# A GFNet-style spectral filter and a mixer MLP on one core: stages pinned to other units, block products in a fifth group, sums moved from GpSimd to VectorE, two loads moved

## The chip, the core and the metric

The kernel runs on one core of a Trainium2 chip. The core has a matrix engine (TensorE, PE in the profile; its weight loads are the row PEld), three engines for elementwise work (VectorE, DVE; ScalarE, ACT; GpSimd, POOL), a queue that issues DMAs (SyncE, SP), an on-chip memory of 128 partitions (SBUF) and eight accumulator banks (PSUM), into which only TensorE multiplies and which GpSimd doesn't reach in this kernel. The metric is the device time of one execution in microseconds; less is better.

## The reference

One input `x` of 2048 tokens by 448 channels is normalised (LayerNorm) and goes through two branches. Their results are added to `x`.

```python
x = A_x
xn = _layernorm(x, axis=-1)
return x + _A_ref(xn, A_w_r, A_w_i) + _B_ref(xn, B_w1, B_w2, B_w3, B_w4)
```

Branch A is a two-dimensional real Fourier transform over tokens and channels, a product with a complex filter of 2048 x 225, and the inverse transform. Branch B is an MLP mixer:

```python
h = _gelu(_layernorm(x, axis=-1) @ w1)            # 448 -> 448
...                                               # four quarters of h shifted by +1, -1, +2, -2 tokens
hs = jnp.concatenate([g0, g1, g2, g3], axis=-1) @ w2
x1 = x + hs
h2 = _gelu(_layernorm(x1, axis=-1) @ w3) @ w4     # 448 -> 1792 -> 448
return x1 + h2
```

## The kernel before, in words

**Numbers.** Every matrix product is made of halves: an fp32 operand is split into a high and a low fp16 part, and three products (high x high, high x low, low x high) are summed in PSUM. The elementwise engines make these splits: ScalarE writes the high part, VectorE the low one.

**Tiling.** The tokens are dealt into 16 blocks of 128 (token index = 16 a + b, block b). Blocks are grouped by four for the first layers of branch B (`GRP`) and by two for its large MLP: group G (0 to 7) holds blocks 2G and 2G + 1, 256 tokens. The 1792 hidden channels are cut into seven pairs of 128, fp = 0 to 6. A *unit* (G, fp) is made of a `front` (first layer: 22 matmuls of 256 columns at L435, then GELU and the split on ScalarE and VectorE, L773 to L777) and a `back` (second layer with w4, added into accumulators over the seven fp).

**Two ways of doing `back`.** A plain unit does 12 matmuls of 448 columns (L811). A *crossed* unit, for the groups listed in `STR` (5, 6, 7 before), does the high x high products plainly (4 matmuls of 448 columns, L811) and takes the two mixed products together as a 2 x 2 block product with seven instead of eight multiplications (Strassen-Winograd): 14 matmuls of 224 columns (L826). For that it needs sums and differences of the blocks of h (`forms`, three VectorE sums a unit, L786 to L788, into `hgm`), of w4 (`w4_forms`, once for each fp, into `w4x` and the end of the w4 tile), and at the end of a group two extra accumulators, which ScalarE copies out (L843), and six group sums (L846, L850). In the last group (G = 7) the units fp = 5 and 6 are plain.

**Branch A in stages.** `do_fold` (x normalised on ScalarE, L578, then four sums on GpSimd, L583 to L586), `step1_in` (split, L594 and L595) and `step1` (transform over a, 24 matmuls for a pair of blocks, L604) go pair by pair of blocks, eight times. `w_scale` takes the largest magnitude of the filter (eight loads, eight `absmax` reductions, L269). Then 16 *chunks* of frequencies pass through `chunk_a` (transform over channels), `chunk_b` (transform over b and product with the filter), `chunk_z` and `chunk_c` (first inverse step). At last the *inverse blocks* run: `gather_u`, `inv_a`, `inv_b`, one for each of the 16 blocks, and `finish` writes the output.

**What sets the order.** The program is written in one order and a planner deals it out to the engines' queues by priorities and its own estimate of times. Each engine then runs its queue strictly in order. Two tools steer the planner. `prio(FILL)` gives work of the large MLP the last priority, so that it fills TensorE wherever nothing else is ready, and `prio(EVAC)` gives what empties its accumulators the first. `behind(key)` pins work to a place: the instructions may be issued only after those that `key` names, ("f", G, fp) for the end of a front's splits, ("m", G, fp) for the last matmul of a back, ("s", n) for the n-th half unit, ("h", g, i) for the transposing DMA of block i of group g. A pin is an earliest place, not a time. The lists at the head of the file hold these places: `FOLD` and `PACE` (start of a pair's fold, its step 1), `WMAX` (the eight maxima), `LATE` (LayerNorm of the last four blocks, `ln2`), `units` with `INV` and `LAG` (inverse blocks). `AH = 2`: fronts run two units ahead of the backs.

Before, the units of G1 and G2 carry the folds, those of G3 and the first of G4 the chunks (a chunk every 7/3 half-unit steps from the start of G3), and the inverse blocks go one to a unit from (4, 4) on, with `inv_b` two units behind `inv_a`. The sums of `w4_forms` run on GpSimd, as do the group sums of G5 and G6; those of G7 run on VectorE.

**Loads.** All DMAs are issued by SP in its own order. The program starts with x, w1, w2 and w3 (w3 in four pieces, `load_w3`, L217 and L219), and `do_fold` loads a pair of x blocks for each fold (L574) into one of four buffers; the fourth is a part of `hgm`, which is free from the start. The `h` of the first layers is turned by transposing DMAs (L492), and so are later operands (L910 into `w4x`, L553 into `x2mem`).

## Time and profile before

| | |
|---|---|
| median of 3 runs | 410.05 us (409.68 to 412.14) |
| profiled execution | 409.72 us |
| its span, first to last instruction | 407.6 us |
| TensorE busy | 401.3 us (98%), 3379 matmuls |
| VectorE, ScalarE, GpSimd busy | 304.2, 268.6, 179.8 us |
| moved by DMA | 49.46 MB, mean 121 GB/s |
| granted TensorE clock | 0.999 |

Times in the rows are microseconds from the first instruction; a row of the groups reads: line, engine, operation, what it writes and reads, shape, count, then busy time and mean nanoseconds of one, then idle time of that engine before it and what ended it. A row of the chain of work that ended last has start, length, and what ran. The busy time of TensorE is modelled at the end of each matmul, so neighbouring matmuls overlap in it; the chain's pieces are cut where the next one starts.

### The profile page before, as it was taken

The numbers are of one execution on the slowest core, as the hardware profiler recorded it, in microseconds if no ns is written. First come the engines' busy times: TensorE is split into PE (matmuls) and PEld (weight loads), VectorE is DVE, ScalarE is ACT, GpSimd is POOL, SyncE is SP. The second block draws the span as 40 slices with busy tenths as digits, with TensorE's granted clock in tenths as the row PEclk, the third lists the DMA queues.
The fourth block names the chain that finished last, engine by engine and source line by source line (L and its number), as shares of the span: only waits on it lengthen the run. The fifth ranks groups of instructions, "written<-read, shape, count | busy, mean of one in ns | idle before, by whom it ended". The sixth has DMA issues, their size and how long they took to land.

```text
span 407.6 us, 8828 instructions
## 1 busy us (share of the span) xinstructions
PE 401.3 (98%) x3379; PEld 296.0 (73%) x3379; DVE 304.2 (75%) x658; ACT 268.6 (66%) x465; POOL 179.8 (44%) x276
## 2 busy tenths in 40 slices
PE   8998999999999999999999999999999999999996
PEld 4553555666767777776888887877788888888885
DVE  5988999899653757894577777763488879889645
ACT  4698993884737865763488888785956566544332
POOL 3889723011197747499243344441231254217100
PEclk9999999999999999999999999999999999999999
DMA  8999999915910375317055666642000022323201
GB/s 282 351 274 198 177 180 261 260 23 109 207 48 0 92 233 175 103 36 170 19 135 146 151 145 151 153 112 60 2 2 2 24 68 75 108 70 112 92 2 45
DMA packets 57209, 49.46 MB, mean 121 GB/s; under 512 B 41312, under 2 KB 52192, under 8 KB 57168
## 3 DMA queue, kind: packets, MB, share of 16 engines
q1 hardware_dynamic: 57168, 48.91, 46.4%
q8 instruction: 26, 0.43, 0.5%
q14 instruction: 15, 0.12, 0.1%
HBM read 35.06 MB, written 3.67 MB: 95 GB/s over the span
## 4 chain that ended last, share of the span: by engine, by line
PE 96%; DMA 2%; ACT 1%; DVE 0%; issue 0%; ACTq 0%
PE pw L435 33%; PE acc L811 24%; PE pw L510 9%; PE pw L465 6%; PE cr L826 4%; PE acc L826 3%; PE pu L707 3%; PE ps L604 3%; PE pp L661 2%; PE pe L727 2%; PE px L678 2%; PE py L749 2%; PE wps L889 2%; DMA h<-hs 2%; PE pta L414 1%; PE end L811 1%
## 5 line engine op out<-in xcount | busy, mean ns | idle before, releaser
L435 PE MATMUL pw<-x2mem,w3p 128*128 128x256 f16 x1232 | 149.7, 272 | 0.0
L435 PEld LDWEIGHTS <-w3p 128*128 128x128 f16 x1232 | 118.7, 98 | 19.4
L811 PE MATMUL acc<-w4p,hf 128*128 128x448 f16 x508 | 107.4, 352 | 0.0
L811 PEld LDWEIGHTS <-hf 128*128 128x128 f16 x532 | 51.5, 98 | 35.5
L777 DVE SCALAR_TENSOR_TENSOR hf<-pw,h,hf 128x512 f16<-128x512 f32 x56 | 41.8, 747 | 36.5 <-ACT hf L776 36.3
L773 ACT ACTIVATE pw<-pw,pe 128x512 f32<-128x512 f32 x56 | 36.7, 656 | 44.8 <-PE pw L435 44.6
L510 PE MATMUL pw<-w2p,h 112*128 112x448 f16 x192 | 39.2, 353 | 1.3 <-DMA h<-hs 1.2
L734 POOL TENSOR_TENSOR e<-e 128x226 f32<-128x226 f32 x16 | 11.1, 696 | 63.7 <-ACT e L731 56.2
L776 ACT ACTIVATE hf<-pw,h 128x512 f16<-128x512 f32 x56 | 38.3, 683 | 1.3
L465 PE MATMUL pw<-w1p,w4x 128*128 128x448 f16 x176 | 34.8, 352 | 0.5 <-DVE h L967 0.5
L510 PEld LDWEIGHTS <-h 112*128 112x128 f16 x192 | 18.4, 98 | 18.0 <-DMA h<-hs 2.2
L688 POOL TENSOR_TENSOR xr<-te 128x450 f32<-128x450 f32 x16 | 15.7, 981 | 34.5 <-DVE te L686 34.5
L465 PEld LDWEIGHTS <-w4x 128*128 128x128 f16 x176 | 17.1, 98 | 16.4 <-ACT w4x L424 0.7
L696 POOL TENSOR_TENSOR zb<-xr,zb 128x450 f16<-128x450 f32 x16 | 16.1, 1009 | 16.8 <-ACT zb L695 16.8
L684 DVE SCALAR_TENSOR_TENSOR te<-px,sc,wc 128x450 f32<-128x450 f32 x16 | 11.0, 685 | 10.6 <-ACT te L683 7.0
L683 ACT ACTIVATE te<-px 64x450 f32<-64x450 f32 x32 | 17.2, 538 | 1.7 <-PE px L678 1.2
L719 ACT ACTIVATE U<-y 113x512 f16<-113x512 f16 x32 | 18.0, 620 | 0.1
L741 ACT ACTIVATE vh<-e 128x448 f16<-128x448 f32 x16 | 9.2, 575 | 13.5 <-DVE e L739 13.3
L731 ACT ACTIVATE e<-pe 128x452 f32<-128x452 f32 x16 | 8.7, 545 | 14.0 <-PE pe L727 11.6
L540 POOL TENSOR_SCALAR y<-xt,nm 128x448 f32<-128x448 f32 x6 | 5.9, 986 | 23.3 <-DMA x2mem<-y 12.9
L711 DVE SCALAR_TENSOR_TENSOR y<-pu,y 113x512 f16<-113x512 f32 x16 | 10.9, 687 | 6.9 <-ACT y L710 6.8
L583 POOL TENSOR_TENSOR xr<-xf 128x452 f32<-128x452 f32 x6 | 6.7, 1125 | 20.6 <-ACT xf L579 10.5
(208 smaller groups left out, 799.0 us busy)
## 6 DMA issues: line engine op xcount, KB each, us to landing
wc<-wf SPq DMA_DIRECT2D x32, 225.0 KB, 3.8
wl<-wf SPq DMA_DIRECT2D x8, 450.0 KB, 3.9
xt<-x SPq DMA_DIRECT2D x3, 896.0 KB, 11.3
w3raw<-w SPq DMA_DIRECT2D x3, 896.0 KB, 14.6
xf<-x SPq DMA_DIRECT2D x6, 448.0 KB, 3.7
xr<-x SPq DMA_DIRECT2D x12, 224.0 KB, 2.5
out<-xr SPq DMA_DIRECT2D x12, 224.0 KB, 2.0
gn<-c_g SPq DMA_DIRECT2D x16, 128.0 KB, 3.2
```

The source lines that it names most:

```text
L435: m = T.matmul(ps_out, wp[:, wi + t, cols], xT[:, xi + t, tok], start=t == 0 and wi + xi == 0, stop=t == 3 and wi == 4)
L465: m = T.matmul(pm[:, :D], xTs[g][:, xi + t, 128 * i:128 * i + 128], w1p[:, wi + t], start=t == 0 and p == 0, stop=t == 3 and p == 2)
L510: m = T.matmul(w2b[b][:, :D], hT[g][:112, 4 * hi + k, o:o + 128], w2p[:, wi, k], start=k == 2 and hi + wi == 0, stop=k == 3 and hi == 1)
L683: i = A.activation(out=e[64 * h:64 * h + 64], in_=px_[64 - 64 * h:128 - 64 * h, :2 * DF], func=AF.Copy)
L688: P.tensor_tensor(out=z, in0=t[:, 0], in1=t[:, 1], op=ALU.add)
L696: P.tensor_tensor(out=zv[1], in0=z, in1=zv[0], op=ALU.subtract)
L719: A.activation(out=U[b][:113, p].rearrange("p q (c k) -> p q c k", c=NC), in_=Y1[:113, p, :, :, b], func=AF.Copy)
L773: A.activation(out=pm, in_=pm, func=AF.Gelu_apprx_tanh, scale=r3)
L776: i = A.activation(out=h[:, 0], in_=pv_, func=AF.Copy, scale=h3)
L777: j = V.scalar_tensor_tensor(out=h[:, 1], in0=pv_, scalar=h3, in1=h[:, 0], op0=ALU.mult, op1=ALU.subtract)
L811: m = T.matmul(to, h[:, hi, 2 * f + i], w4p[0][:, wi, 2 * fp + f, r], start=fp == s and f == 0 and hi + wi == 0, stop=fp == e and f == 1 a ...
L826: m = T.matmul(to, h[:, hi, slot] if slot < 4 else g[:, hi, slot - 4], w4f[fp][k][wi], start=k in (0, 6) and fp == 0 and hi == 0, stop=hi ...
```

## The change

- `STR` becomes (4, 5, 6, 7): the seven units of G4 use block products too, with their `forms`, the two extra accumulators and the group sums.
- `w4_forms` runs on VectorE, four operations for each fp instead of six on GpSimd, and is pinned behind the split of block 13 instead of behind the folds of block 0 and block 14. The group sums of G5 and G6 (and G4) run on VectorE.
- Folds, step 1 and the maxima are pinned to earlier units (all within G1 and the first of G2, from (0, 5) on). The chunks start behind (2, 0) instead of at the start of G3; groups 1 to 5 are now one run of the generator. `LATE` moves from (2, 2) to (2, 5) to (3, 5) to (4, 1) and `ln2` of the last blocks is written behind the chunks. The inverse blocks start at (4, 0), six units for five blocks, with `inv_b` three units behind and a third buffer for `vh`; the gathers of U are pinned; the order of blocks is 12 to 15, then 0 to 11.
- The fourth piece of w3 is loaded behind the transpose of ("h", 0, 3) instead of in the first burst. The x pairs of the folds are loaded behind ("h", 3, 3) at the earliest, up to four pairs ahead of their fold. The loads of the maxima are dealt out among the folds.

```diff
-PACE = [(0, 6), (1, 1), (1, 2), (1, 4), (1, 5), (2, 0), (2, 1), (2, 3)]
-FOLD = [(0, 5), (1, 0), (1, 1), (1, 3), (1, 4), (1, 6), (2, 0), (2, 2)]
+PACE = [(0, 6), (1, 0), (1, 1), (1, 2), (1, 4), (1, 5), (1, 6), (2, 0)]
+FOLD = [(0, 5), (0, 6), (1, 0), (1, 1), (1, 3), (1, 4), (1, 5), (1, 6)]
-WMAX = [(1, 4), (1, 5), (2, 0), (2, 0), (2, 1), (2, 2), (2, 3), (2, 4)]
-LATE = [(2, 2), (2, 3), (2, 4), (2, 5)]
+WMAX = [(1, 0), (1, 0), (1, 2), (1, 3), (1, 4), (1, 5), (1, 6), (2, 0)]
+LATE = [(3, 5), (3, 6), (4, 0), (4, 1)]
-STR = (5, 6, 7)
-INV, LAG = 4, 2
+STR = (4, 5, 6, 7)
+LAG = 3
...
-    load_w3([2, 3])
+    load_w3([2])
...
+    def load_fold(b0):
...
+        with behind("h", 3, 3):
+            SY.dma_start(X[:, :, 0:D], xv[:, b0:b0 + 2])
+        Xs[b0] = f, X
...
-                    (V if G == 7 else P).tensor_tensor(out=o, in0=x, in1=y, op=ALU.add)
+                    V.tensor_tensor(out=o, in0=x, in1=y, op=ALU.add)
...
-                    (V if G == 7 else P).tensor_tensor(out=to[i], in0=to[i], in1=cross[:, 1 - i], op=ALU.add)
+                    V.tensor_tensor(out=to[i], in0=to[i], in1=cross[:, 1 - i], op=ALU.add)
...
-        P.tensor_tensor(out=t3, in0=b[1][1], in1=b[0][1], op=ALU.add)
-        for i in range(2):
-            P.tensor_tensor(out=t1[i], in0=b[0][0][:, i], in1=b[0][1][:, i], op=ALU.subtract)
-            P.tensor_tensor(out=t2[:, i], in0=b[1][1][:, i], in1=t1[i], op=ALU.subtract)
-        P.tensor_tensor(out=t4, in0=b[1][0], in1=t2, op=ALU.subtract)
+        for o, x, y, op in ((t3, b[1][1], b[0][1], ALU.add), (t1, b[0][0], b[0][1], ALU.subtract),
+                            (t2, b[1][1], t1, ALU.subtract), (t4, b[1][0], t2, ALU.subtract)):
+            V.tensor_tensor(out=o, in0=x, in1=y, op=op)
...
+    with behind("h", 0, 3):
+        load_w3([3])
...
-    mlp([1, 2], ahead=AH, tags=("mm", "tr"))
+    gen = steps(range(1, 6), ahead=AH, tags=["mm", "tr"] * 4 + ["mm"] * 27)
+    while ("m", 2, 0) not in after:
+        run(gen, len(slots))
+    run(gen, len(slots))
+    wm, wl = pc.tile([128, 8], F32, name="wm"), stage("wl", 8 * DF, 1)
+    for b in range(0, 8, 2):
+        load_fold(b)
     for b in range(0, NB, 2):
+        if b == 0:
+            w_max(wm, wl, 0)
+        elif b < 10:
+            load_fold(b + 6)
+        if b < 14:
+            w_max(wm, wl, 1 + b // 2)
         do_fold(b)
...
-            with behind("fold", 0 if fp < 2 else 14):
+            with behind("x", 13):
                 w4_forms(fp)
-    ln2(range(12, 16), [A] * 4, LATE)
-    with behind("X", 14):
-        wm = w_scale()
     close("pfd")
-    with behind("m", 2, 5):
+    with behind("m", 2, 0):
         w_scale_end(wm)
...
-    gen, s0 = steps(range(3, 6), ahead=AH), len(slots)
+    s0 = len(slots)
...
+    ln2(range(12, 16), [A] * 4, LATE)
...
-    bs = [*range(12, 16), *range(8, 12), *range(8)]
-    units = [(G, fp) for G in range(4, 8) for fp in range(7)][INV:]
+    bs = [*range(12, 16), *range(12)]
+    units = [(G, fp) for G in range(4, 8) for fp in range(7)]
+    ahead = [(3, 6)] + units
+    at_unit = [6 * n // 5 for n in range(16)]
...
-                gather_u(bs[n])
-                with behind("m", *units[n]):
+                with behind("f", *ahead[at_unit[n]]):
+                    gather_u(bs[n])
+                with behind("m", *units[at_unit[n]]):
                     inv_a(bs[n])
             if n:
-                with behind("m", *units[min(n - 1 + LAG, 20 - INV)]):
+                with behind("m", *units[min(at_unit[n - 1] + LAG, 20)]):
```

More of the change, by code (lines that the diff above doesn't have):

```diff
@@ L569, in body, with do_fold @@
     folds = {}
-    def do_fold(b0):
+    Xs = {}
+    def load_fold(b0):
         f = xf_buf[b0 // 2 % 4]
         X = f.rearrange("p b s d -> p (b s d)")[:, 0:2 * D + 2].rearrange("p (b d) -> p b d", b=2)
-        after["X", b0] = (SY.dma_start(X[:, :, 0:D], xv[:, b0:b0 + 2]).ins,)
+        with behind("h", 3, 3):
+            SY.dma_start(X[:, :, 0:D], xv[:, b0:b0 + 2])
+        Xs[b0] = f, X
+    def do_fold(b0):
+        f, X = Xs.pop(b0)
         with behind("f", *FOLD[b0 // 2]):
@@ L611, in body, with w_max @@
     sc = pc.tile([128, 4], F32, name="sc")
-    def w_scale():
-        wm = pc.tile([128, 8], F32, name="wm")
-        t = stage("wl", 8 * DF, 1)
-        for c in range(8):
-            h = t[:, 4 * DF * (c % 2):4 * DF * (c % 2) + 4 * DF]
-            SY.dma_start(h, wf.rearrange("c (p r) n -> (c p) (r n)", r=8)[:, 4 * DF * c:4 * DF * (c + 1)])
-            with behind("f", *WMAX[c]):
-                absmax(wm[:, c:c + 1], h)
-        return wm
+    def w_max(wm, t, c):
+        h = t[:, 4 * DF * (c % 2):4 * DF * (c % 2) + 4 * DF]
+        SY.dma_start(h, wf.rearrange("c (p r) n -> (c p) (r n)", r=8)[:, 4 * DF * c:4 * DF * (c + 1)])
+        with behind("f", *WMAX[c]):
+            absmax(wm[:, c:c + 1], h)
     def w_scale_end(wm):
@@ L687, in chunk_b @@
         z = xr[:, 2 * DF * (c % 2):2 * DF * (c % 2) + 2 * DF]
-        P.tensor_tensor(out=z, in0=t[:, 0], in1=t[:, 1], op=ALU.add)
+        after["z", c] = (P.tensor_tensor(out=z, in0=t[:, 0], in1=t[:, 1], op=ALU.add).ins,)
         zs[c] = z
@@ L739, in inv_a @@
         V.tensor_tensor(out=v[:, 225:336], in0=u[:, 1, 0, 1:112], in1=u[:, 1, 1, 1:112], op=ALU.add)
-        vh = pv.tile([128, 2, D], F16, tag="vh", bufs=2, name=f"vh{b}")
+        vh = pv.tile([128, 2, D], F16, tag="vh", bufs=3, name=f"vh{b}")
         A.activation(out=vh[:, 0], in_=v, func=AF.Copy)
```

4 lines of the change are left out of this document (2 added, 2 removed).

## The prediction, on record before the result

> **What bounds the kernel now.** I read the first part of the page first, then the list of all waits of TensorE.
>
> ```profile
> span 407.6 us, 8828 instructions
> PE 401.3 (98%) x3379; PEld 296.0 (73%) x3379; DVE 304.2 (75%) x658; ACT 268.6 (66%) x465; POOL 179.8 (44%) x276
> ```
> ```profile
> PE wps L889 <- DVE x2mem L188: 1.2, 1, 1.2
> PE pw L510 <- DMA h<-hs: 1.2, 1, 1.2
> PE pw L465 <- DVE h L967: 0.5, 1, 0.5
> ```
>
> TensorE is busy for 401.3 of 407.6 us and the list of its waits has three entries, 2.9 us in all: the warm-up at the very start, the product with w1 that follows it, and one wait at 32.07 us (its row is below, with the loads). After that the list names nothing. A 98% alone would prove little, since the matmuls' ends are modelled. So the next view is the chain that ended last, cut to two stretches: G0 with plain second products (L811 alone) and G7 with block products (L811, then L826).
>
> ```profile
> 104.93 2.40 PE pw L435 x22
> 107.33 2.27 PE acc L811 x12
> 109.60 2.40 PE pw L435 x22
> ```
> ```profile
> 392.90 2.40 PE pw L435 x22
> 395.31 0.76 PE acc L811 x4
> ...
> 397.40 2.40 PE pw L435 x22
> ```
>
> Each piece starts where the one before ended, and every matmul takes its own streaming time: 22 of 256 columns in 2.40 us (109 ns each), 12 of 448 columns in 2.27 us (189 ns each). The kernel is bound by TensorE's stream of matmuls. A change can win only by making that stream shorter or by removing the early stalls, and it can lose only by making a stream that is now gapless wait.
>
> **The change part by part.**
>
> *Block products in G4.* This is the only edit that changes TensorE's work. A plain unit's second product takes 2.27 us. A unit with block products runs from 395.31 to 397.40, so 2.09 us: 0.76 for four matmuls of 448 columns and 1.33 for fourteen of 224 columns (95 ns each, half of 189). That is 0.18 us a unit and **1.26 us** for the seven units of G4. G4 has no other matmuls added.
>
> Here a rule of the Trainium skill speaks against the edit. By the page "TensorE: Matmul & The Clock Gate", section "Back-to-back issue gap", a stream of weight loads and matmuls sustains about 81 ns a matmul at 128 columns and about 131 at 512, so halving the width saves much less than half. Between these, an estimate is 94 ns at 224 columns and 123 at 448, by which a plain unit would take 1.47 us and a block unit 1.80, and G4 would lose 2.3 us instead of winning 1.26. The trace disagrees: 189 ns at 448 columns and 95 at 224 in the rows above.
>
> *The two loads.* The queue of SP at the start, the two loads' time to landing, the transposes' (all of L492, then the one in the chain), who waited for them, and what the DMA engines moved in 40 slices of 10.2 us:
>
> ```profile
> 11.21 0.47 SPq L219 DMA_DIRECT2D w3raw<-w  x1
> 11.72 0.59 SPq L574 DMA_DIRECT2D hgm<-x  x1
> 25.04 6.80 SPq L492 DMA_TRANSPOSE h<-hs  x3
> 31.94 2.65 SPq L492 DMA_TRANSPOSE h<-x2mem  x2
> ```
> ```profile
> w3raw<-w SPq DMA_DIRECT2D x1, 448.0 KB, 18.3
> hgm<-x SPq DMA_DIRECT2D x1, 448.0 KB, 18.9
> ```
> ```profile
> DMA to landing us min/median/max: 3.0/3.5/7.0
> ```
> ```profile
> 26.60 6.30 DMA h<-hs
> ```
> ```profile
> 32.07 7.56 PE L510 MATMUL pw<-w2p,h 112*128 112x448 f16 x36 [1.17 <-DMA h<-hs]
> 39.47 0.73 PE L465 MATMUL pw<-w1p,w4x 128*128 128x448 f16 x3
> ```
> ```profile
> ACT hs L488 <- DMA h<-hs: 1.7, 1, 1.7
> ```
> ```profile
> GB/s 282 351 274 198 177 180 261 260 23 109 207 48 0 92 233 175 103 36 170 19 135 146 151 145 151 153 112 60 2 2 2 24 68 75 108 70 112 92 2 45
> ```
>
> The last quarter of w3 and one pair of x blocks are issued at 11.21 and 11.72 and land 18.3 and 18.9 us later, at about 29.5 and 30.6. The first transposes of h are issued from 25.04 on, behind them, and take up to 7.0 us to land, where the median is 3.5. Their issue is held up too: three take 6.80 us, where two later ones take 2.65, so about 2.8 us too long. TensorE waits for them 1.17 us at 32.07, and its next 36 matmuls take 7.56 us where 36 times 0.189 and a last tail of 0.16 make 6.97, so 0.59 us more goes in short waits. These 1.76 us are what the edit can win here. With both loads gone from that place the backlog ends some 2.6 us sooner (0.9 MB at the 351 GB/s of the second slice).
>
> What is late next: the w3 quarter now enters SP's in-order queue behind the transpose h(0,3) and ahead of the next transposes of h and of x (w4x), and costs them 0.47 us of issue and about 1.3 us of transfer (448 KB at 351 GB/s). Those for w4x have no slack: TensorE's L465 began at 39.47, as the transposes landed. So of 2.8 us won in that queue, 1.3 to 1.8 are given back, and TensorE can run ahead by 1.0 to 1.5 us. I take **1.3 us**, with bounds of 1.76 and of -1.3: nothing, if the waits move on to the w4x transposes, and less by the load's own transfer, if it passes ahead of transposes that have gained nothing. ScalarE's wait of 1.7 for the same transpose frees up too, so the engines behind it can follow. The other x loads go out after h(3,3); the pair moved from 11.72 is read past 130 us, and the second x2 transposes, which it may pass on SP, are read by G1 past 119 us. Nothing waits for that.
>
> *Folds, chunks, inverse moved forward.* TensorE executes the same matmuls in another order, so by itself this is worth nothing. It costs if the other engines can't keep up in the denser stages. The busy times by stage (folds with G1 and G2; chunks with G3 and G4; G5; G6), then the prices:
>
> ```profile
> core 0: us, PE busy (x) PEld busy (x) DVE busy (x) ACT busy (x) POOL busy (x), PEclk, DMA share, GB/s
> 119.00:190.00 71.00, 71.00 (x641) 54.46 (x639) 49.71 (x65) 49.26 (x87) 52.08 (x58) 1.00 0.38 109
> 195.00:286.00 91.00, 91.00 (x934) 73.97 (x933) 62.36 (x104) 70.73 (x128) 33.14 (x34) 1.00 0.47 118
> 291.00:331.00 40.00, 40.00 (x385) 32.80 (x384) 33.85 (x83) 24.01 (x44) 10.62 (x15) 1.00 0.06 19
> 331.00:371.00 40.00, 40.00 (x390) 33.77 (x388) 34.39 (x80) 21.60 (x38) 15.05 (x21) 1.00 0.26 82
> ```
> ```profile
> L777 DVE SCALAR_TENSOR_TENSOR hf<-pw,h,hf 128x512 f16<-128x512 f32 x56 | 41.8, 747 | 36.5 <-ACT hf L776 36.3
> L595 DVE TENSOR_TENSOR xh<-xf,xh 128x452 f16<-128x452 f32 x12 | 11.8, 1017 | 3.1 <-ACT xh L594 3.1
> L609 DVE TENSOR_TENSOR y<-ps,y 128x512 f16<-128x512 f32 x16 | 10.4, 680 | 1.8 <-ACT y L608 1.8
> L269 DVE TENSOR_REDUCE wm<-wl 128x1 f32<-128x900 f32 x8 | 8.6, 1080 | 1.1 <-DMA wl<-wf 1.1
> L786 DVE TENSOR_TENSOR hgm<-hf 128x512 f16<-128x512 f16 x19 | 9.6, 505 | 0.9
> L846 DVE TENSOR_TENSOR x2mem<-x2mem 128x224 f32<-128x224 f32 x4 | 1.6, 392 | 0.6 <-ACT x2mem L843 0.4
> L850 DVE TENSOR_TENSOR x2mem<-x2mem 128x448 f32<-128x448 f32 x2 | 1.2, 617 | 0.0
> ```
> ```profile
> 119.25 1.34 PE ps L604 x24
> ```
>
> In the fold stage a pair of blocks now meets one unit in eight places between the end of G0 and the second unit of G2. A unit with a pair holds TensorE for 2.40 + 2.27 + 1.34 (24 matmuls in the chain's row) = 6.0 us. VectorE's share of it is 0.75 + 2 x 1.02 + 2 x 0.68 + 1.08 = 5.2 us, or 6.3 where two maxima fall into one unit, which happens once. That is 87%, and the LayerNorm of the last four blocks leaves this stage, so I cost it at nothing. TensorE's own backlog hides it: first layers run two units ahead of their second products, which is 2 x 4.67 us.
>
> In the chunk stage VectorE now sits idle for 91.0 - 62.4 = 28.6 us. The forms of w4, 28 sums of 448 columns, come from GpSimd; at no more than L786's 0.505 us each they take up to 14.1 us, at the back of the priorities. They fit; cost nothing. If every one of them were to hold a chunk's chain up, 14 us would be the price.
>
> In G4 to G6 VectorE gets the forms of h for G4 (three sums a unit, at most 1.5 us) and the group sums (4 x 0.392 + 2 x 0.617 = 2.8 us a group, three times, two of them from GpSimd). Before, G5 and G6 hold 34 us of VectorE in 40 us each, about 7 inverse blocks among them. After, 16 blocks are spread over three groups at one per 1.2 units, so a group holds 5.8. With some 3 us a block (the busy 34 less seven units at 0.75 + 1.5 over seven blocks gives 2.6), a group's VectorE goes to about 34 - 1.2 x 2.6 + 2.8 = 33.7, while TensorE's time falls to some 38. That is 88% after 85%: the same, nearly. At the boundary from G4 to G5 the accumulators must be emptied while one first layer (2.40 us) runs. Two evacuations of 0.68 us, which wait for no sum, fit; if the four small sums went ahead of the second one, 1.57 us more, TensorE would wait about 1 us, once.
>
> *The sum.* 409.72 us is the profiled execution's own time, 2.1 above its span. 409.72 - 1.26 - 1.3 = 407.2. The median of the runs shown is 0.33 higher, so I say **407.3 us**.
>
> **The rivals.**
>
> *The loads win nothing.* The w4x transposes are late instead, or the queue's order puts the w3 quarter where it holds h up. For it speaks that L465 had no slack at 39.47. Time: 409.72 - 1.26 = 408.5.
>
> *VectorE falls behind (slower).* Place: the chunk stage and the start of G4, where the w4 sums, the group sums and the chunks' evacuations share one in-order queue, with GpSimd's own sums beside them. Another sum of VectorE, L786, has a mean of 505 ns and a longest of 949 beside GpSimd.
>
> ```profile
> L786 DVE TENSOR_TENSOR hgm<-hf x19: 409/426/949, 291.7 to 393.0; 128x512 f16<-128x512 f16 x19
> ```
>
> If all 28 sums took 0.95 us they would need 26.6 of the 28.6 idle us, and each late evacuation would reach TensorE once its lead of two units is used up. Against it: that lead, and the gapless 40 us stretches with VectorE at 85%. It decides from about 95% busy on; with 0.95 - 0.43 (the median) = 0.5 us lost in about half of the 28 places on top of one boundary's 1 us, TensorE loses 8 us: about 415. A milder course, a quarter of that, ends at 409.
>
> The Trainium skill's page "SBUF — State Buffer", section "Who interferes with whom", says that a VectorE instruction with two SBUF inputs contends with a GpSimd one that reads SBUF, which is what these 949 ns look like; it also means that sums taken off GpSimd free VectorE elsewhere.
>
> *Narrow matmuls are bound by their weight loads.* Rows: a load takes 98 ns, and a block unit has 18 of them, 1.76 us of its 2.09.
>
> ```profile
> L811 PEld LDWEIGHTS <-hf 128*128 128x128 f16 x532 | 51.5, 98 | 35.5
> ```
>
> If loads and matmuls stopped overlapping in G4's fourteen narrow ones, these would take 14 x (95 + 98) = 2.70 us instead of 1.33, and G4 would add 7 x 1.19 = 8.3 us: 416.8 with the loads' gain. The page on TensorE named above goes that way with its 81 ns. G7's rows exclude it nearly: the same code there runs at 95 ns.
>
> *The change doesn't move what it says.* The pins are earliest times only; if folds and chunks end up where they were, TensorE's sum is the same and the time is the forecast's.
>
> **How the numbers follow.** Chances: forecast 0.50 (406.6 to 408.0), loads win nothing 0.27, VectorE behind 0.16 (409 to 418), narrow matmuls 0.02, and 0.05 for more than forecast (the loads' 1.76 in full and the 0.5 us that L465 waits for L967, which give 406.2, and short early waits that the list doesn't name). The range of 406.2 to 411.5 takes in the first two and the milder part of the third. A measurement of this kernel can tell about 1%, 4.1 us, from no change. Faster than 406.0 holds 0.04; slower than 414.1 holds 0.10, half of the third case and the fourth; the rest, 0.86, lies within.
>
> **What would show it.** Right: G4's units at 2.09 us in the chain, no wait of TensorE past 70 us, the wait for h gone or below 0.5 us, transposes of h landing within 4 us, VectorE below 90% in G4 to G6. Wrong: waits of L826 or L811 for hgm, w4x or accumulators, of L661 or L604 for VectorE, or a wait of L465 for w4x near 38 us. A stall in the fold stage would be the step I trust least, since its 87% is a sum of means.

## The result, and the profile after

The changed kernel takes 414.69 us (median of 6 runs, 413.66 to 416.99), the kernel before 410.28 us beside it. The ratio is 1.0096, 95% interval 1.007 to 1.0122: slower by about 4 us, where 407.3 was forecast. The profiled execution of after takes 414.07 us, its span is 412.0. Where the granted clock of a run fell to half for a few microseconds, its mean is 0.991 to 0.996 instead of 1.0 and the time is 1 to 3 us longer, so medians and profiled spans of one kernel can differ by that much; one run at a mean of 0.754 (522.63 us, see the late sums below) is left out.

The first part of the page of after, then the list of TensorE's waits (line, what it waited for: us in total, times, longest):

```profile
span 412.0 us, 8952 instructions
PE 400.9 (97%) x3421; PEld 299.7 (73%) x3421; DVE 321.8 (78%) x725; ACT 268.4 (65%) x467; POOL 137.9 (33%) x222
```
```profile
PE pw L510 <- DMA h<-x2mem: 1.8, 1, 1.8
PE pw L435 <- DVE hf L780: 1.3, 2, 1.0
PE wps L892 <- DVE x2mem L188: 1.2, 1, 1.2
PE ps L611 <- ACT hf L779: 1.2, 1, 1.2
PE ps L611 <- ACT pw L776: 0.7, 1, 0.7
PE pw L510 <- DVE xt L517: 0.6, 1, 0.6
PE pw L465 <- DVE h L968: 0.5, 1, 0.5
...
```

(two more of 0.2 each). Three waits became nine, and 2.9 us became 7.7. (Lines below the diff's first insertions moved by a few: L777 is now L780, L604 is L611, L826 is L829, L846 and L850 are L849 and L853.) The matmuls themselves did what was forecast. The chain that ended last, in G4:

```profile
304.53 2.40 PE pw L435 x22
306.93 0.76 PE acc L814 x4
...
310.20 2.40 PE pw L435 x22
```

Between 306.93 and 310.20 lie the block unit and 1.18 us of an inverse block (0.57 at L752 and 0.61 at L730 in that chain), which leaves 2.09.

To set the gain against the losses I took all starts of TensorE's timeline and split the span into *streaming* (each matmul at the time its width takes in the gapless stretches: 189 ns at 448 columns, 109 at 256, 95 at 224) and the rest, by place:

| us | before | after | what waits in after |
|---|---|---|---|
| streaming | 395.4 | 394.2 | |
| 0 to 20 | 3.8 | 3.8 | start |
| 20 to 40 | 2.2 | 2.2 | L510 for a transpose of h, at 37 (before: at 32) |
| 80 to 100 | 0.1 | 0.9 | L510 for L517, at 89 |
| 160 to 180 | 0.0 | 2.5 | L611, step 1 of the last folds, twice |
| 280 to 300 | 0.1 | 1.3 | several of 0.1 to 0.25, LayerNorm of the last blocks late |
| 340 to 345 | 0.1 | 1.2 | L435, third front at the boundary of G5 and G6 |

-1.2 + 0.8 + 2.5 + 1.2 + 1.1 = 4.4 us, the difference of the spans (412.0 - 407.6). What the rows leave out, 5.9 us, is alike in both; 3.5 of it is the end of the program behind the start of the last matmul.

The largest one first. TensorE, ScalarE and VectorE in after's timeline (start, length, engine and line, in brackets the idle time before it and what ended it):

```profile
168.26 0.83 PE L611 MATMUL ps<-csm,xh 128*128 128x128 f16 x12 [0.72 <-ACT pw L776]
170.31 0.83 PE L611 MATMUL ps<-csm,xh 128*128 128x128 f16 x12 [1.21 <-ACT hf L779]
```
```profile
160.79 0.57 ACT L601 ACTIVATE xh<-hgm 128x452 f16<-128x452 f32 x1
```
```profile
158.41 4.49 DVE L933 TENSOR_TENSOR w4x<-w4p 128x448 f16<-128x448 f16 x12
162.83 0.68 DVE L933 TENSOR_TENSOR w4p<-w4p 128x448 f16<-128x448 f16 x2
163.43 0.68 DVE L933 TENSOR_TENSOR w4x<-w4p,w4x 128x448 f16<-128x448 f16 x2
...
166.60 0.61 DVE L602 TENSOR_TENSOR xh<-hgm,xh 128x452 f16<-128x452 f32 x1
...
167.44 0.67 DVE L616 TENSOR_TENSOR y<-ps,y 128x512 f16<-128x512 f32 x1
...
168.34 0.61 DVE L602 TENSOR_TENSOR xh<-hgm,xh 128x452 f16<-128x452 f32 x1
...
169.49 0.67 DVE L616 TENSOR_TENSOR y<-ps,y 128x512 f16<-128x512 f32 x1
```

ScalarE has written the second high part of the last pair of folds by 161.4. The low parts (L602) stand in VectorE's queue behind sixteen w4 sums in a row and a few more, and run at 166.60 and 168.34. Behind each of them stands L616, which takes the low half of step 1's result for a block of the pair before and so empties one of the two accumulator banks that step 1 uses. L616 ends at 168.11 and 170.16, and TensorE's two groups of step 1 start 0.15 us behind them, but more than 1 us behind the ends of the two L602: the bank came last. (In the kernels below that keep this pin and the sums on VectorE, the distance is 0.14 or 0.15 us too.) The releaser that the list names (ScalarE) is not the one that came last here; the starts show it. The busy times of these stretches (the columns are the engines in the order PE, PEld, DVE, ACT, POOL) show why a stage's mean hid it:

```profile
119.00:166.00 47.00, 47.00 (x438) 36.59 (x437) 37.10 (x58) 33.21 (x62) 28.02 (x28) 1.00 0.43 129
```
```profile
157.10:171.10 14.00, 12.07 (x115) 9.11 (x114) 14.00 (x35) 6.35 (x11) 2.25 (x4) 1.00 0.13 34
```

79% of 47 us, and 100% of the 14 us that count. VectorE's stage average was below my bound while a batch in its queue cost TensorE 2.5 us.

### The profile page after: what moved, and what is told of

It is laid out like the page before. It is cut to its first block, busy times and chain, and to the rows that moved or that the text cites. A ratio compares the mean times of both kernels' runs of the same rounds, so it can differ in the third digit from the quotient of the medians.

```text
span 412.0 us, 8952 instructions
## 1 busy us (share of the span) xinstructions
PE 400.9 (97%) x3421; PEld 299.7 (73%) x3421; DVE 321.8 (78%) x725; ACT 268.4 (65%) x467; POOL 137.9 (33%) x222
## 4 chain that ended last, share of the span: by engine, by line
PE 77%; DMA 7%; DVE 6%; ACT 5%; issue 1%; POOL 0%; SPq 0%; ACTq 0%; DVEq 0%
PE pw L435 27%; PE acc L814 19%; PE pw L465 6%; PE pw L510 4%; PE cr L829 3%; DMA x2mem<-y 3%; PE ps L611 3%; PE acc L829 3%; PE pp L664 2%; PE pu L710 2%; PE px L681 2%; PE py L752 2%; PE pe L730 2%; DMA h<-x2mem 1%; DMA x2mem<-w 1%
## 5 line engine op out<-in xcount | busy, mean ns | idle before, releaser
L435 PE MATMUL pw<-x2mem,w3p 128*128 128x256 f16 x1232 | 150.1, 272 | 1.3 <-DVE hf L780 1.3
L435 PEld LDWEIGHTS <-w3p 128*128 128x128 f16 x1232 | 119.0, 98 | 19.1 <-issue 1.7
L814 PE MATMUL acc<-w4p,hf 128*128 128x448 f16 x452 | 96.4, 352 | 0.0
L814 PEld LDWEIGHTS <-hf 128*128 128x128 f16 x476 | 46.2, 98 | 31.3 <-issue 0.2
L780 DVE SCALAR_TENSOR_TENSOR hf<-pw,h,hf 128x512 f16<-128x512 f32 x56 | 41.8, 746 | 34.5 <-ACT hf L779 34.0
L510 PE MATMUL pw<-w2p,h 112*128 112x448 f16 x192 | 38.9, 352 | 2.4 <-DMA h<-x2mem 1.8
L737 POOL TENSOR_TENSOR e<-e 128x226 f32<-128x226 f32 x16 | 12.9, 808 | 75.5 <-ACT e L734 64.4
L510 PEld LDWEIGHTS <-h 112*128 112x128 f16 x192 | 18.7, 98 | 18.8 <-DMA h<-x2mem 2.2
L829 PEld LDWEIGHTS <-hgm 128*128 128x128 f16 x208 | 19.9, 98 | 0.2
L829 PE MATMUL cr<-w4x,hgm 128*128 128x224 f16 x138 | 19.4, 259 | 0.0
L829 PEld LDWEIGHTS <-hf 128*128 128x128 f16 x156 | 15.0, 98 | 4.7
L538 ACT ACTIVATE y<-xt,nm 128x448 f32<-128x448 f32 x10 | 6.4, 664 | 14.1 <-DMA x2mem<-y 11.8
```

Of the source, the lines that this page charges most:

```text
L435: m = T.matmul(ps_out, wp[:, wi + t, cols], xT[:, xi + t, tok], start=t == 0 and wi + xi == 0, stop=t == 3 and wi == 4)
L510: m = T.matmul(w2b[b][:, :D], hT[g][:112, 4 * hi + k, o:o + 128], w2p[:, wi, k], start=k == 2 and hi + wi == 0, stop=k == 3 and hi == 1)
L780: j = V.scalar_tensor_tensor(out=h[:, 1], in0=pv_, scalar=h3, in1=h[:, 0], op0=ALU.mult, op1=ALU.subtract)
L814: m = T.matmul(to, h[:, hi, 2 * f + i], w4p[0][:, wi, 2 * fp + f, r], start=fp == s and f == 0 and hi + wi == 0, stop=fp == e and f == 1 a ...
L829: m = T.matmul(to, h[:, hi, slot] if slot < 4 else g[:, hi, slot - 4], w4f[fp][k][wi], start=k in (0, 6) and fp == 0 and hi == 0, stop=hi ...
```

## The experiments

Times are medians; ratios are to the kernel before on the same chip, with 95% intervals. "Rest" is the time not streaming, as in the table above.

### The sums of w4 in VectorE's queue

Later: the sums may be issued only behind the last evacuation of step 1.

```diff
-        V.tensor_tensor(out=y[1], in0=src, in1=y[0], op=ALU.subtract)
+        after["y", b] = (V.tensor_tensor(out=y[1], in0=src, in1=y[0], op=ALU.subtract).ins,)
...
-            with behind("x", 13):
+            with behind("y", 15):
                 w4_forms(fp)
```

> The changed kernel with one edit: the 28 sums of w4 stay on VectorE but are pinned behind the last evacuation of step 1 (block 15) instead of behind the split of block 13. Theory (a queue in the wrong order): the 2.5 us that TensorE loses at 167 to 171 us come from 16 of these sums standing in VectorE's queue ahead of the splits and evacuations of the last two pairs. Then L611 no longer waits there, the span falls by 2.3 to 2.6 us (412.0 to about 409.5), and nothing grows elsewhere. Rival (VectorE is too full for the denser order): the wait comes back within the chunk stage, since 8.4 us of sums are still to be done there; span between 411 and 412.

Measured: 412.58 us, 1.0028 (1.0004 to 1.0051), span 408.9. The rest at 160 to 180 us falls from 2.5 to 0.1, and nothing comes for it in the chunk stage. The span falls by more than that, 3.1 us, since the wait at 89 us is absent in this run (more on it below). The sums' place was the cause, not their amount.

On GpSimd: the same four operations and the same pin, with the engine as the only edit.

```diff
-            V.tensor_tensor(out=o, in0=x, in1=y, op=op)
+            P.tensor_tensor(out=o, in0=x, in1=y, op=op)
```

> The changed kernel with the w4 sums on GpSimd (the same four operations for each pair), pinned as in the changed kernel. Theory (a queue in the wrong order): with the sums out of VectorE's queue the waits at 167 to 171 us go, as they did when the sums were pinned later; GpSimd's sums of about 1.05 us each, 29 us, run beside the chunks and may stretch VectorE's sums with two inputs in SBUF, and the chunks' own GpSimd sums come later. Span 409 to 410. Rival (the fold stage is too dense whatever stands in that queue): the waits stay, span 411.5 to 412.5.

Measured: 418.59 us, 1.0194 (1.0162 to 1.0227), span 415.3. The wait at 167 is gone, and a larger one stands at 108 us: the instructions that the pin names are on ScalarE and VectorE, and in GpSimd's queue the sums now stand at 89.7 us and later, beside the small steps of the second LayerNorm on VectorE. TensorE's, then VectorE's timeline of this kernel, and the window behind the wait (after the engines' columns stands the granted clock):

```profile
112.90 3.92 PE L814 MATMUL acc<-w4p,hf 128*128 128x448 f16 x10 [4.68 <-DVE hf L780]
```
```profile
107.93 0.95 DVE L303 TENSOR_TENSOR nqb<-nib 128x4 f32<-128x4 f32 x1
108.92 0.16 DVE L304 TENSOR_TENSOR nqb<-nqb,vb 128x4 f32<-128x4 f32 x1
...
112.11 0.74 DVE L780 SCALAR_TENSOR_TENSOR hf<-pw,h,hf 128x512 f16<-128x512 f32 x1
```
```profile
112.90:117.50 4.60, 4.60 (x15) 2.14 (x16) 4.57 (x6) 1.20 (x3) 3.44 (x5) 0.50 0.18 33
```

Operations on four elements a partition take 0.16 us or 0.95 beside GpSimd; L780 runs late, TensorE waits 4.7 us and then runs at half its clock for 4.6 us. The sums run earlier here as well as on another engine, so this run doesn't compare the engines alone. That VectorE can take the sums without a wait of TensorE is shown by the run before it: moving them there was not the mistake, releasing them there in the fold stage was.

### The staging buffer of the last LayerNorm

`ln2` of the last four blocks comes in two halves, and both halves use staging buffer 0. ScalarE's, then SP's timeline of after:

```profile
277.67 1.23 ACT L538 ACTIVATE y<-xt,nm 128x448 f32<-128x448 f32 x2 [3.55 <-DMA x2mem<-y]
```
```profile
273.02 2.89 SPq L553 DMA_TRANSPOSE x2mem<-y  x2
...
280.37 2.57 SPq L553 DMA_TRANSPOSE x2mem<-y  x2
```

ScalarE stands for 3.55 us until the first half has been transposed out of the buffer, and the gathers of U and the evacuations of first layers stand behind it. The second half in the other buffer:

```diff
-            w = stage(f"y{b0 + m}", 8 * 448, 0 if pins else (b0 + m) // 2 % 2, F16)
+            w = stage(f"y{b0 + m}", 8 * 448, (b0 + m) // 2 % 2, F16)
```

> The changed kernel with the second half of the last LayerNorm (blocks 14 and 15) in the other staging buffer, so that ScalarE doesn't stand 3.5 us behind the transposes of blocks 12 and 13. Theory: the short waits of TensorE between 281 and 292 us (1.1 us together) come from ScalarE's late gathers and front evacuations behind that wait; span about 411.0. Rival: ScalarE and VectorE are busy there with seven gathers in a row anyway, and the waits stay; span 411.8 to 412.2.

Measured: 413.79 us, 1.0073 (1.0051 to 1.0095), span 410.3. The rest at 280 to 300 falls from 1.3 to 0.1; the second transposes go out at 277.28 instead of 280.37. Then this edit and the later w4 sums together:

> The changed kernel with two edits: the w4 sums behind the last evacuation of step 1, and the second half of the last LayerNorm in the other staging buffer. Theory (separate causes): both savings add up, 2.4 and 1.2 us, and the wait at 89 us, which came and went without an edit, stays away; what is left is the 1.2 us at the boundary from G5 to G6 and the 1.9 us at 37 us. Span 407.6 to 408.4, so within 0.3% of the kernel before in time. Rival (VectorE too full): the second edit's gain is lost with the w4 sums in the chunk stage; span 409 or more.

Measured: 409.81 us, 0.9991 (0.9969 to 1.0012), span 407.5. Two edits make up for the whole loss: 2.5 and 1.2 us are theirs, and the 0.8 at 89 us is absent in this run, as it is in both runs with one of the edits alone. Its list of waits keeps the transposes (1.8 at L510) and the boundary (1.0 at L435).

### The two loads

Both as before:

```diff
+    load_w3([2, 3])
-        with behind("h", 3, 3):
-            SY.dma_start(X[:, :, 0:D], xv[:, b0:b0 + 2])
+        SY.dma_start(X[:, :, 0:D], xv[:, b0:b0 + 2])
-    with behind("h", 0, 3):
-        load_w3([3])
```

> The changed kernel with both loads where they were: the fourth quarter of w3 in the first burst and the x pairs free to go as early as their buffers are. Theory: the w3 quarter only moved TensorE's wait from 32 us to 37 us at the same length (1.9 us each), so that part is worth nothing, while the x pair loaded at 75 us delays the transposes of the second MLP LayerNorm and costs the 0.8 us wait at 89 us: span 411.2, with the wait at 32 us back. Rival: the two loads are worth the 1.3 us forecast and the wait at 37 us has another cause: span 413 or more.

Measured: 414.56 us, 1.0103 (1.0055 to 1.0151), span 411.7. The wait at 37 us goes and the one at 32 us comes back (1.35 us), while the wait at 89 us is absent: as the change makes them, the two moves are worth nothing. SP's timeline of after shows where the gain went:

```profile
25.02 4.25 SPq L492 DMA_TRANSPOSE h<-hs  x3
29.37 1.34 SPq L492 DMA_TRANSPOSE h<-x2mem  x1
30.77 0.58 SPq L219 DMA_DIRECT2D w3raw<-w  x1
31.45 1.26 SPq L492 DMA_TRANSPOSE h<-x2mem  x1
32.80 3.05 SPq L492 DMA_TRANSPOSE h<-hs  x1
36.03 5.29 SPq L913 DMA_TRANSPOSE w4x<-x  x4
```

The first transposes are on time now (the first three take 4.25 us to issue, 6.80 before). Then the w3 quarter, at 30.77, stands ahead of two more transposes of h. In the chain that ended last the next one is this piece:

```profile
31.45 5.71 DMA h<-x2mem
```

It takes 5.71 us from its issue to landing, and TensorE waits for it until 37.21. The transposes of w4x start at 36.03 (36.17 before).

Next, the quarter further back and the x pair behind the transposes of LayerNorm b2 (on top of the two edits above, as are all kernels below unless another base is named):

```diff
-        with behind("h", 3, 3):
+        with behind("b2"):
...
-    with behind("h", 0, 3):
-        load_w3([3])
...
+    with behind("t", 2):
+        load_w3([3])
```

> The kernel of e6_both with the two loads moved on: the fourth quarter of w3 behind the transposes of x for the third group instead of behind h(0,3), and the x pair behind the second MLP LayerNorm. Theory (the wait for h is a matter of what stands ahead in the DMA queue): the 1.9 us wait at 32 or 37 us goes, span 1.3 to 1.9 us below that of e6_both, so about 406.2, below the kernel before. Rival: the next transposes, those of x, had no slack and become the wait, or the late quarter of w3 holds up its own squares; span the same as e6_both within 0.4 us.

Measured: 411.5 us, 1.0022 (1.0007 to 1.0037), span 410.0. The rest at 20 to 40 falls to 0.3, but 40 to 100 rises from 0.3 to 4.6: the quarter, issued at 39.52, now stands ahead of the next transposes of h, and what is made of w3 is late (ScalarE waits 4.43 us for the quarter). The other way round, the w3 quarter in the first burst again and the x pair alone behind b2:

```diff
-    load_w3([2])
+    load_w3([2, 3])
...
-        with behind("h", 3, 3):
+        with behind("b2"):
...
-    with behind("h", 0, 3):
-        load_w3([3])
```

> The kernel of e6_both with the fourth quarter of w3 back in the first burst, and the x pair not loaded before the second MLP LayerNorm's transposes are issued. Theory (what counts is how many bytes stand ahead of the first transposes of h): with the x pair's 448 KB gone from the burst the transposes start some 1 us sooner than in the kernel before, and no load stands among them; TensorE's 1.9 us around 32 us shrink to 0.3 to 1.0, span 0.9 to 1.6 us below e6_both: about 406.2, faster than the kernel before. Rival (the time to landing of the transposes is their own, or the engines behind set the wait): the wait stays at 1.5 us or more, span 407.1 to 407.6.

Measured: 408.16 us, 0.995 (0.9932 to 0.9967), span 405.7; the rest at 20 to 40 is 0.3 and nothing comes after it. So it is enough to take the x pair out of the burst, with all of w3 in it. The same single edit on the kernel before:

```diff
-        after["X", b0] = (SY.dma_start(X[:, :, 0:D], xv[:, b0:b0 + 2]).ins,)
+        with behind("b2"):
+            after["X", b0] = (SY.dma_start(X[:, :, 0:D], xv[:, b0:b0 + 2]).ins,)
```

> The kernel before with one edit: the x pairs of the folds aren't loaded before the second MLP LayerNorm's transposes are issued, so that the pair loaded at 11.7 us leaves the first burst (w3 stays whole in it). Theory: as in e10_w3_first the wait around 32 us shrinks from 1.9 to 0.3 to 1.0 us, span 406.0 to 406.7. Rival: no change, 407.4 to 407.8.

Measured: 407.87 us, 0.9938 (0.9918 to 0.9958), span 406.2. TensorE's longest waits in it (the two others are of 0.4 and 0.2):

```profile
PE wps L890 <- DVE x2mem L188: 1.2, 1, 1.2
PE pw L465 <- DVE h L968: 0.5, 1, 0.5
...
```

The wait for h is gone. One pin is worth 2.5 us by the ratio and 1.4 by the spans. Whether taking out the w3 quarter and leaving the x pair would do as well no run shows.

The wait at 89 us points to the x pair too. SP's timeline of after, then that of the kernel with the w3 quarter in the first burst and the pin on b2:

```profile
74.78 0.57 SPq L577 DMA_DIRECT2D hgm<-x  x1
76.84 5.56 SPq L553 DMA_TRANSPOSE x2mem<-y  x2
```
```profile
74.84 3.16 SPq L553 DMA_TRANSPOSE x2mem<-y  x2
78.05 0.60 SPq L577 DMA_DIRECT2D hgm<-x  x1
```

Ahead of the two transposes, the load stretches their issue from 3.16 to 5.56 us. ScalarE's next step of the LayerNorm waits 1.76 us for the buffer that they read, and L517 behind it is late. No kernel without the load in that place has this wait. But it is small and unsteady: 0.8 us in after, none in the runs with the w4 sums later or the other staging buffer, though the load stood there in both. So the load goes with it and doesn't always bring it; why it comes and goes is open.

### Block products in the fifth group

The kernel with the two edits (409.81 us), and G4 plain again:

```diff
-STR = (4, 5, 6, 7)
+STR = (5, 6, 7)
```

> The kernel of e6_both without block products in G4 (plain second products there, no forms of h and no group sums for G4): the price of the block products by themselves. Theory: TensorE's stream is 1.2 us longer and nothing else changes; span 1.0 to 1.4 us above e6_both. Rival (block products cost G4 as much in waits as they save): span within 0.5 us of e6_both, or below it.

Measured: 410.8 us, 1.0009 (0.9989 to 1.0029), span 409.2. Streaming is 395.4 again, 1.2 more, and 0.5 is a wait at 89 us of the kind above. The medians differ by 1.0, and the two intervals overlap. By the streaming the block products win their 1.2 us, and no wait is added for them. The page "TensorE: Matmul & The Clock Gate" of the Trainium skill, section "Back-to-back issue gap", would have had them lose time by its sustained rate; these runs don't agree with it (95 ns at 224 columns, weight loads included).

### The boundary of G5 and G6

VectorE's timeline of after, where TensorE's L435 starts at 345.16 after 1.01 us of waiting:

```profile
342.09 0.77 DVE L849 TENSOR_TENSOR x2mem<-x2mem 128x224 f32<-128x224 f32 x1
342.79 0.26 DVE L739 TENSOR_TENSOR e<-e 128x113 f32<-128x113 f32 x1
...
343.83 0.61 DVE L853 TENSOR_TENSOR xt<-xt,x2mem 128x448 f32<-128x448 f32 x1
344.37 0.74 DVE L780 SCALAR_TENSOR_TENSOR hf<-pw,h,hf 128x512 f16<-128x512 f32 x1
```

Three first layers run in a row here with two accumulator banks. The third needs the bank of the first, which L780 empties, and L780 stands behind the group sums (L849, L853) and the differences of an inverse block (L739 to L742). Which of the two groups matters? First, on the changed kernel, the group sums back on GpSimd:

```diff
-                    V.tensor_tensor(out=o, in0=x, in1=y, op=ALU.add)
+                    (V if G == 7 else P).tensor_tensor(out=o, in0=x, in1=y, op=ALU.add)
...
-                    V.tensor_tensor(out=to[i], in0=to[i], in1=cross[:, 1 - i], op=ALU.add)
+                    (V if G == 7 else P).tensor_tensor(out=to[i], in0=to[i], in1=cross[:, 1 - i], op=ALU.add)
```

> The changed kernel with the group sums of G4, G5 and G6 on GpSimd again (G7's stay on VectorE). Theory: the 1.2 us that TensorE waits for the low half of a front at 344 us, at the boundary from G5 to G6, come from group sums ahead of it in VectorE's queue; they go, span about 410.8, and the boundary from G4 to G5 stays without a wait. Rival: the wait is set by the inverse block beside it, or GpSimd's sums slow VectorE's own by as much; span within 0.4 us of 412.0.

Measured: 418.5 us, 1.0185 (1.0145 to 1.0225), span 415.1. The boundary's wait doubles, from 1.2 to 2.5. GpSimd's, then VectorE's timeline of this kernel:

```profile
345.15 2.28 POOL L853 TENSOR_TENSOR xt<-xt,x2mem 128x448 f32<-128x448 f32 x2
```
```profile
341.15 0.27 DVE L742 TENSOR_TENSOR e<-e 128x111 f32<-128x111 f32 x1
...
346.36 1.19 DVE L742 TENSOR_TENSOR e<-e 128x111 f32<-128x111 f32 x1
347.48 0.74 DVE L780 SCALAR_TENSOR_TENSOR hf<-pw,h,hf 128x512 f16<-128x512 f32 x1
```

VectorE is rid of the sums, but beside GpSimd's two differences of 0.27 us take 1.2 each, and L780 is later than before. The page "SBUF — State Buffer" of the Trainium skill, section "Who interferes with whom", names this pair of engines as the one that contends; the trace agrees, by 0.27 against 1.19. In this run the matmuls after the waits at 168 to 170 also ran at half clock, which costs another 1.4 us.

Then the inverse blocks moved away from the boundary, first alone, then with the loads mended:

```diff
-    at_unit = [6 * n // 5 for n in range(16)]
+    at_unit = [0, 1, 2, 3, 4, 6, 7, 8, 9, 10, 11, 12, 14, 15, 16, 18]
```

> The kernel of e6_both with the inverse blocks shifted so that none starts behind (5, 6), the last unit of G5: one block starts a unit earlier there. Theory (VectorE's queue at the boundary holds the two evacuations, the six group sums and an inverse block ahead of the split that three first layers in a row wait for): without the block's five sums, 1.8 us, the wait of 1.2 us goes; span 406.3 to 406.8. Rival (the group sums alone are too much there): the wait stays above 0.8 us, span 407.2 or more.

> The edits of e10_w3_first and e11_boundary together. If both theories hold: span about 405.3, time 407.4, 0.7% below the kernel before. If neither: 407.5.

Measured: 411.26 us, 1.0017 (0.9997 to 1.0036), and 408.31 us, 0.9951 (0.9933 to 0.9969). Neither is a gain over its base (409.81 and 408.16), and the wait at the boundary is unchanged at 1.2: the places given were earliest places, and VectorE's order there stayed the same. So these two runs don't test the theory. (The first is longer than its base by matmuls at half clock behind the wait at 37 us; see the last section.) Next, the group sums written later in the program, after the second unit of the next group, on the kernel with the loads mended (408.16) and on the changed one:

```diff
+                def sums():
+                    for o, x, y in (...):
+                        V.tensor_tensor(out=o, in0=x, in1=y, op=ALU.add)
...
+                    late.append(lambda: (sums(), add(0), add(1)))
+            if fp == 1 and late:
+                late.pop()()
```

> The kernel of e10_w3_first with the group sums of G4, G5 and G6 written behind the second unit of the next group instead of at the end of their own; the evacuations stay where they are. Theory (it is the six sums, 2.8 us, that stand ahead of the first front's split in VectorE's queue at the boundary from G5 to G6): the wait of 1.2 us goes; span 404.4 to 404.8, time about 406.7, 0.8% below the kernel before. Rival (the inverse blocks' work alone fills the queue there): the wait stays above 0.6 us, span 405.2 or more.

> The changed kernel with that edit alone. Theory: the wait at 344 us goes, all others stay; span 410.8 (or 410.0 if the wait at 89 us is absent). Rival: span 411.6 to 412.2 with the wait in place.

Measured: 408.15 us, 0.9951 (0.9933 to 0.997), and 415.19 us, 1.0137 (1.0082 to 1.0191). The wait is 1.2 in both: a later place in the program didn't move the sums in VectorE's queue either. (The second is longer than after by matmuls at half clock behind the waits at 168.) So the last run pins them there:

```diff
             if fp == 1 and late:
-                late.pop()()
+                with behind("f", G, 1):
+                    late.pop()()
```

> This kernel is the one whose group sums are written late (the staging buffer and the w4 sums' place mended, the w3 quarter in the first burst, the x pairs behind the transpose of LayerNorm b2), with the group sums of G4 to G6 also pinned behind the splits of the second front of the next group, so that they must stand behind that front's L780-type split in VectorE's queue. It tells what the third front at the G5 to G6 boundary waits for. Theory A: the four small sums and two adds (about 2.8 us of VectorE) ahead of the first front's low split are the cause; the wait of 1.17 us at about 339 us falls below 0.3, the span falls from 406.0 to about 405 and the time from 408.15 to about 407.2. Theory B: the inverse blocks' own sums (the differences of e, 1.0 us a block, vh and xt) hold the split up; the wait stays above 0.6 us, span above 405.5, time 408 or so. A third way: the sums now stand ahead of the forms of h of the third unit, and block products wait instead, at 343 to 348 us; time 408 to 409.

Measured: 406.8 us (406.28 to 407.53), 0.9912 (0.9881 to 0.9943), span 404.9. VectorE's timeline of this kernel (its L850 is L849 of after), then TensorE's longest waits (the two others are of 0.3 and 0.2):

```profile
335.77 0.66 DVE L739 TENSOR_TENSOR e<-e 128x113 f32<-128x113 f32 x1
...
336.91 0.74 DVE L780 SCALAR_TENSOR_TENSOR hf<-pw,h,hf 128x512 f16<-128x512 f32 x1
...
339.75 0.38 DVE L850 TENSOR_TENSOR x2mem<-x2mem 128x224 f32<-128x224 f32 x1
```
```profile
PE wps L904 <- DVE x2mem L188: 1.2, 1, 1.2
PE pw L465 <- DVE h L980: 0.5, 1, 0.5
...
```

The differences of the inverse block still stand ahead of L780, the sums behind it, and the wait is gone. Taking the sums out was enough; whether taking the differences out would have been, no run shows, since none moved them. TensorE's list names no wait past 12 us, and the kernel beats both the one before and the one changed. Most of its 0.9% against the kernel before is the x pair's pin, which wins 0.6% there by itself (407.87 us). Beyond that pin, the whole repaired change is worth 1.1 us by the medians (the intervals of the two ratios overlap), about what the block products save.

## Why the prediction was wrong

**The bound held.** TensorE's stream bounds the kernel: the differences in streaming and in the named waits add up to the difference of the spans, and the experiments moved the span by what waits grew or shrank, and in four of them by matmuls at half clock behind a wait as well.

**Block products: right.** -1.26 was forecast; streaming fell by 1.2, and G4's units take 2.09 us.

**The loads: forecast -1.3, came out at 0, and +0.8 at 89 us.** The rival "loads win nothing" held, but in its second form: not the transposes for w4x were late, but the remaining ones of h behind the w3 quarter. The step "costs them 0.47 us of issue and about 1.3 us of transfer" failed. By the chain the transpose behind the quarter took 5.71 us from issue to landing, against a median of 3.5 before. I had also put the old wait down to both loads together; the run with one pin on the kernel before shows that it goes when the x pair alone is taken out. The step "Nothing waits for that", of the x pair ahead of the second x2 transposes, looked only at who reads their result. The writer of the buffer that they read from was waiting, though TensorE lost time by it in some runs only.

**Folds, chunks and inverse moved: forecast 0.** "I cost it at nothing", by 87% of VectorE in the fold stage, failed together with "at the back of the priorities" for the w4 sums. I counted the sums into the chunk stage's idle 28.6 us; released behind the split of block 13, they were in VectorE's queue ahead of the last pair's splits and of the evacuations (L616) that TensorE waited for. Their size was fair (0.30 us from start to start, at most 0.505 assumed). The lead of two units did not hide a batch of some 6 us in the queue, because step 1 stands in TensorE's own order and the units behind it can't pass. It cost 2.5. A wait of L604 (now L611) for VectorE, one of the prediction's signs of being wrong, is what came. The prediction named the fold stage as the step it trusted least, for the right reason, and gave it no price.

**LayerNorm of the last blocks: not priced.** I wrote only that it leaves the fold stage. In its new place both halves meet in one staging buffer: 1.2.

**Group sums: "TensorE would wait about 1 us, once" at the boundary, costed at 0.** The size was right (1.1 to 1.2), the place was G5 to G6 and not G4 to G5, and what waited was the low split of a first layer and not the evacuation of the accumulators. So the agreement in size is chance. It should have stood in the sum.

**The rival "VectorE falls behind"** had the right mechanism, an in-order queue shared by sums and evacuations, and a share of VectorE's time as its condition ("from about 95% busy on"), which was wrong: 79% in the stage was enough, and in 291 to 331 us VectorE was busy for 37.34 of 40.00 us (93%, where the prediction had 88%) with a rest of 0.1. Its places were wrong too: the waits came in the fold stage and between G5 and G6, not in the chunk stage and at the start of G4. Of the 5.6 us lost, 2.5 + 1.1 at two places are this queue's; the 1.2 and, as far as known, the 0.8 came from staging buffers, which no rival had. The narrow matmuls bound by weight loads are excluded.

## What to carry to other kernels

When work is moved to an engine with idle time, don't compare sums with shares of a stage: find the instruction that would stand right behind the batch in that engine's in-order queue, and who waits for it. A load is priced by what is issued behind it: the same pair of x blocks cost 1.4 to 2.5 us ahead of transposes and nothing behind them, and a buffer's next writer waits as much as its reader does. A change of many parts that ends 4 us slower held a gain of 7.5 us over itself, by the two ratios: one pin for the w4 sums, one buffer, two loads and one pin for the group sums took 1.0096 to 0.9912. Set the repaired kernel also against the old one with the same repair: most of the gain was one pin that needed none of the change.

## What was not expected of the hardware

A short wait can cost more than itself. After 4.68 us without work TensorE's granted clock was 0.50 for 4.6 us (the windows above). One wait of 1.84 us was followed by slow matmuls in one kernel, and 1.79 us at the same place in another was not. TensorE's timeline of the kernel with the inverse blocks moved (without the loads), then of after:

```profile
37.27 3.37 PE L510 MATMUL pw<-w2p,h 112*128 112x448 f16 x12 [1.84 <-DMA h<-x2mem]
```
```profile
37.21 2.44 PE L510 MATMUL pw<-w2p,h 112*128 112x448 f16 x12 [1.79 <-DMA h<-x2mem]
```

The granted clock, read window by window, shows what differs. In all 17 traces it changes only at whole multiples of 3.413 us after the moment at which it first became full (4.50 us in the first kernel, 5.33 in after). In the first kernel the whole wait falls into one such window, 35.22 to 38.63, in which TensorE is busy for 1.56 of 3.41 us, and the clock is 0.50 from 38.63 to 42.05. In after the wait lies across two windows, with 2.78 and 2.26 us busy, and the clock stays at 1.00. Waits add up within a window: the 0.7 and 1.2 us of step 1 leave 1.53 us busy in the run with the group sums on GpSimd, and 3.41 us at half clock follow; in after the same two waits lie in two windows (2.61 and 2.25 busy), and nothing follows. Of six windows with 1.56 us busy or less up to the last matmul, five were followed by half clock; the sixth (1.51) was not, and none with 1.60 or more was. So the limit lies near half of a window, and these traces don't settle it exactly. The first full clock came at 4.2 to 7.2 us, differently in each trace, so whether one and the same wait costs some 1.7 us more than itself can change from run to run. Of the 52 runs of the five kernels that have neither the wait at 37 us nor those at 168, none has a mean clock below 0.999.

The Trainium skill's page "TensorE: Matmul & The Clock Gate", section "What's actually happening", gives an idle window of about 3.4 us for the drop to half; the halving and the window's length agree (0.50 and 3.413 us), but here 1.85 us of idle time within a window was enough.
